# The end of token group 0 in another order, and three loads of group 3 issued sooner, in a kernel for block-wise attention with decay and an MLP

## The chip, the cores and the metric

The kernel runs on one core of one Trainium2 chip. The metric is the device time of one execution in microseconds (us); lower is better. Engines are named as in the profile: PE is TensorE, DVE VectorE, ACT ScalarE, POOL GpSimd, SP SyncE. POOL and SP each issue DMAs in the order of the program; POOL's go through the software queue (queue 0), SP's through the hardware queue (queue 1).

## What is computed

Attention with decay over 4 sequences of 768 tokens, 8 heads of 64, in blocks of 64 tokens with a running state per head, then an MLP with an exact GELU on the 3072 tokens (512 to 2048 and back to 512).

```python
for b in range(nb):                                   # nb = 12 blocks of 64 tokens
    intra = einsum('bhic,bhjc->bhij', qb, kb) * Dmask[None]
    intra = einsum('bhij,bhjd->bhid', intra, vb)
    inter = einsum('bhid,bhde->bhie', qb * lam_pow[None], kv_state)
    out[:, :, sl] = intra + inter
    kv_state = lam_block * kv_state + einsum('bhsd,bhse->bhde', kb * rev_pow[None], vb)
x = out.transpose(0, 2, 1, 3).reshape(3072, 512)
h = x @ w_in
out = (0.5 * h * (1 + erf(h / sqrt(2)))) @ w_out
```

## The kernel before

**Tiling.** A chunk is 128 tokens of one sequence (two blocks), a group is the same 128 tokens of all four sequences: chunks 4g to 4g+3 are group g, and there are six groups. While PE computes the MLP of group g, it also does the attention of group g+1 (in part g+2), in pieces put between blocks of the MLP. Nothing is scheduled automatically: each engine does its instructions in the order in which the program writes them.

**The MLP** (`mlp`, from L430) is a list of named blocks. `a`, `b`, `m` and `l` blocks are the first matmul (L439, L456) with GELU on ACT; `p0` to `p15` are the second matmul, four matmuls of 512 columns each (L478). In group 0 the `p` blocks go round the four output tiles, so that the four tiles end in `p12`, `p13`, `p14` and `p15`, and ACT copies each out (L467). In group 1 `a0` to `a3` use only chunks 4 and 5 and are half as wide.

**The attention of a chunk n** needs, in this order:
- loads of k and q (`load`, L71, POOL; for chunks 4 to 7 q comes for two chunks at once) and of V for a whole group in four DMAs (`load_blocks`, L106, POOL). They change the type from fp32 to bf16. A load waits for the semaphore that the load eight issues before it uses too.
- the transposes of k and q, tile `kqT`: for chunks 4 to 7 by PE in `both_transposed` (L248 and L252, 20 small matmuls into one PSUM bank; then a copy of the k half by DVE, L254, and of the q half by ACT, L255, one after the other, since both read one bank); from chunk 8 on by SP's DMA transposes in `request` (L259, L260).
- V times the decay, tile `vd`: `decay_v`, L282, on POOL.
- k in an order by blocks, tile `k2`: two copies `same` (L269) and two `other` (L273), on various engines. `values(n)` is `decay_v` and `same` on POOL, `keys(n)` is `other` on DVE.

**A visit(f, d)** (L349 and on) issues, interleaved pair by pair, chunk d's scores (8 pairs) and then its states (8 pairs, from `vd` and `k2`) and chunk f's outputs (16 pairs, from `kqT`, the masked scores `sm`, V, the state and the mid state `mid`). All matmuls are recorded at L347. After it DVE does the mask of d (L293), the first sum for the state (L308), then a copy to `mid` (L310 on ACT for chunks 4 to 7, L312 on DVE later), and "empties" f: x_t gets the outputs times a decay (L339). With `first=True` the emptying of f stands ahead of d's mask on DVE, else after the first sum.

**Order.** `run_blocks` (L519) walks the blocks; `ahead` and `plan_of` name what is put ahead of a block, on whichever engines. The lines around the change are those of group 0's second matmul (L590 to L602) and of `plan_of(1)` (L622 to L645), with n = 8: `m9` visit(None, 8), `m14` visit(8, 9), `p4` visit(9, 10), `p9` visit(10, 11), `p14` visit(11, 12). In group 2 `m0` has values(13), `m7` visit(12, 13), and `m15` visits chunk 13 with 14 and 15. `fetch` (L613) issues the loads of k and q of two chunks; where the first of these begins a group, V of that group too (L618).

Buffers: ten for k, ten for q from chunk 8 on, three for V of a group, six each for `kqT`, `vd`, `k2` and for output tiles, four PSUM banks for scores, states, outputs and transposes in turn.

Of the kernel before, what the change touches and what calls it, by code (L numbers as in the profile page):

```python
# [15 lines left out]
def kernel(  # L16
# [10 lines left out]
    nc = tc.nc  # L27
# [26 lines left out]
    def bank(shape, dtype, tag, name):  # L54
        return ps.tile(shape, dtype, tag=tag, name=name, bufs=BANKS[tag])

    def half(i):
        return slice(i * 64, (i + 1) * 64)
# [157 lines left out]
    live = {}  # L216
# [25 lines left out]
            dst, src = (t.rearrange(f"d hp ({o}) -> d hp p j", j=2) for t, o in ((c.qT, "p j"), (t_ps, "j p")))  # L242
        (nc.scalar.copy if eng is nc.scalar else eng.tensor_copy)(dst, src)

    def both_transposed(c):
        t_ps = bank([128, 2, HP, C], BF16, "at", "t_ps")
        for hp in range(HP):
            nc.tensor.transpose(t_ps[:, 0, hp, :], c.k[:, 2 * hp:2 * hp + 2, :], ident)  # L248
        for hp in range(HP):
            for j in range(2):  # L250
                for hi in range(2):
                    nc.tensor.transpose(t_ps[half(hi), 1, hp, half(j)], c.q[:, 2 * hp + hi, j, :],  # L252
                                        ident[half(0), half(0)])
        nc.vector.tensor_copy(c.kT, t_ps[:, 0])  # L254
        nc.scalar.copy(c.qT.rearrange("d hp (p j) -> d hp p j", j=2),  # L255
                       t_ps[:, 1].rearrange("d hp (j p) -> d hp p j", j=2))

# [27 lines left out]
    def scores(c):  # L285
        sc = c.sc = bank([128, 2, HP, L], F32, "at", "sc_ps")
        return [[(sc[half(hi), u, hp, :], c.kT[half(hi), hp, u * L:(u + 1) * L],
                  c.qT[half(hi), hp, u * L:(u + 1) * L], True) for hi in range(2)]
                for u in range(2) for hp in range(HP)]

    def mask(c):
        c.sm = work_pool.tile([128, 2, HP, L], BF16, tag="sm", name="sm")
        nc.vector.tensor_mul(c.sm, c.sc, dmask)  # L293

    def states(c):
        kv = c.kv = bank([128, 2, HP, D], F32, "at", "kv_ps")
        us = range(2) if c.g < NG - 1 else range(1)
        return [[(kv[half(hi), u, hp, :], c.k2[half(hi), u, hp, :], vd[c.n][half(hi), u, hp, :], True)
                 for hi in range(2)] for u in us for hp in range(HP)]
# [20 lines left out]
    def outputs(c, tag="at"):  # L320
        o = c.o = bank([128, HP, C], F32, tag, "o_ps")
        pairs = []

        def inter(u, s):
            for hp in range(HP):
                pairs.append([(o[half(1 - hi), hp, u * L:(u + 1) * L], s[half(hi), hp, :],
                               c.qT[half(hi), hp, u * L:(u + 1) * L], False) for hi in range(2)])

        inter(0, state[c.n])
        for u in range(2):  # L330
            for hp in range(HP):
                pairs.append([(o[half(1 - hi), hp, u * L:(u + 1) * L], c.v[half(hi), u, hp, :],
                               c.sm[half(hi), u, hp, :], False) for hi in range(2)])
        inter(1, c.mid)
        pairs[0] = [(*p[:3], True) for p in pairs[0]]
        return pairs

    def empty(c):
        nc.vector.tensor_mul(xT[c.g][:, :, c.b * C:(c.b + 1) * C], c.o, lam_o)  # L339

    def issue(*lists):

        for i in range(max(map(len, lists))):
            for pairs in lists:
                if i < len(pairs):
                    for out_, lhsT, rhs, start in pairs[i]:
                        nc.tensor.matmul(out_, lhsT, rhs, start=start, stop=True, skip_group_check=True)  # L347

    def visit(f, d, first=False):  # L349
        f, d = (live[n] if n is not None else None for n in (f, d))  # L350
        lists = []
        if d:
            kv = states(d)
            lists.append(scores(d) + kv)
        if f:
            lists.append(outputs(f))
        issue(*lists)
        if d is None or f and (first or f.g > 1):
            empty(f)
            f = None  # L360
        if d:
            mask(d)
            next_states(d, lambda: f and empty(f))
# [197 lines left out]
    def request(*ns):  # L561
        for n in ns:
            dma_transposes(live[n])

    def same(n, eng):
        by_block(live[n], eng, None)

    def other(n):
        by_block(live[n], None, nc.scalar)

    def ahead_of_group_1():

        for n in range(B, 2 * B):
# [20 lines left out]
        "p2": [lambda: both_transposed(live[4])],  # L594
        "p8": [lambda: visit(None, 4)],
        "p10": [lambda: both_transposed(live[5]), lambda: other(5)],
        "p12": [lambda: visit(4, 5), lambda: other(6)],
        "p13": [lambda: both_transposed(live[6])],
        "p14": [lambda: same(7, nc.vector)],
        "p15": [lambda: both_transposed(live[7]), lambda: other(7), lambda: visit(5, 6, first=True),  # L600
                lambda: request(8)],
    })  # L602


# [1 line left out]
    def values(n):  # L606
        decay_v(n)
        by_block(live[n], nc.gpsimd, None)
# [4 lines left out]
    def fetch(*ns):  # L613
        ns = [n for n in ns if n < NG * B]
        for n in ns:
            ask(f"k{n} q{n}")
        if ns and ns[0] % B == 0 and ns[0] > 2 * B:
            ask(f"V{ns[0] // B}")  # L618
        for n in ns:
            begin(n)  # L620

    def plan_of(g):  # L622
        if g == 1:
            n = 2 * B
            return {
                "a0": [lambda: values(n), lambda: request(n + 1), lambda: store_held(slice(0, 2))],
                "a2": [lambda: visit(n - 2, n - 1, first=True)],
                "b2": [lambda: fetch(n + 2, n + 3)],
                "m4": [lambda: visit(n - 1, None)],
                "m5": [lambda: keys(n), lambda: request(n + 2, n + 3), lambda: store_held(slice(2, B))],  # L630
                "l0": [lambda: values(n + 1)],
                "m9": [lambda: visit(None, n)],
                "m10": [lambda: values(n + 2)],
                "m11": [lambda: keys(n + 1)],
                "m14": [lambda: visit(n, n + 1)],
                "m15": [lambda: values(n + 3), lambda: fetch(n + 4, n + 5), lambda: request(n + 4, n + 5)],
                "p0": [lambda: keys(n + 2)],
                "p4": [lambda: visit(n + 1, n + 2)],
                "p5": [lambda: fetch(n + 6, n + 7), lambda: values(n + 4)],
                "p6": [lambda: keys(n + 3), lambda: request(n + 6, n + 7)],  # L640
                "p9": [lambda: visit(n + 2, n + 3)],
                "p11": [lambda: keys(n + 4)],
                "p13": [lambda: fetch(n + 8, n + 9)],
                "p14": [lambda: visit(n + 3, n + 4)],
            }  # L645
        if g == NG - 1:
            return {}
        n = (g + 1) * B
        if g == 2:
            return {  # L650
                "m0": [lambda: values(n + 1)],
                "m2": [lambda: keys(n + 1)],
                "m7": [lambda: visit(n, n + 1)],
                "m8": [lambda: values(n + 2), lambda: request(n + 4, n + 5)],
                "m10": [lambda: keys(n + 2), lambda: values(n + 3)],
                "m13": [lambda: keys(n + 3)],
                "m15": [lambda: visits([n + 1], [n + 2, n + 3], ["mo1"])],
                "p0": [lambda: fetch(n + 6, n + 7), lambda: values(n + 4)],
                "p2": [lambda: request(n + 6, n + 7), lambda: values(n + 5)],
                "p8": [lambda: keys(n + 4), lambda: keys(n + 5)],  # L660
                "p12": [lambda: visits([n + 2, n + 3], [n + 4, n + 5], ["mh", "mh"]), lambda: values(n + 6)],
            }

        def each(act, *ns):
            for n in ns:
                if n < NG * B:
                    act(n)

        return {
            "m0": [lambda: fetch(n + 4, n + 5), lambda: values(n + 3)],  # L670
            "m4": [lambda: keys(n + 2), lambda: keys(n + 3)],
            "m8": [lambda: each(request, n + 4, n + 5)],
            "m12": [lambda: visits([n, n + 1], [n + 2, n + 3], ["mo0", "mo1"]), lambda: each(values, n + 4)],
            "p0": [lambda: fetch(n + 6, n + 7), lambda: each(values, n + 5)],
            "p4": [lambda: each(request, n + 6, n + 7)],
            "p8": [lambda: each(keys, n + 4, n + 5)],
            "p12": [lambda: visits([n + 2, n + 3], [n + 4, n + 5], ["mh", "mh"]), lambda: each(values, n + 6)],
        }
# [34 lines left out]
```

## Time and profile before

| What | Value |
|---|---|
| Median of 3 runs | 211.13 us (209.91 to 211.71) |
| The profiled execution | 210.78 us |
| Its span, first to last instruction | 208.9 us |
| PE busy | 197.0 us, 94% |
| POOL busy | 104.6 us, 50% |
| DMA packets, queue 0 and queue 1 | 74080 and 21152 |
| Granted TensorE clock | 0.999 |

The profile records one execution. A row of the timeline has the start, the time taken, the engine, the line, the operation, what it writes and reads, how often, and in brackets how long the engine sat idle before it and what ended that. A row of the waits has who waited for whom, the total in us, how often, and the longest. A row of the DMA queues has packets, megabytes, and the time of the packets as a share of the 16 DMA engines' time. Matmuls overlap, so the distance between two starts tells more than their busy times. Some matmul records are missing: where a row has one matmul fewer than the program, a distance that looks doubled is no stall.

### The profile page before, as it was taken

How to read it: one execution, taken by the hardware profiler on the slowest of the kernel's cores; microseconds unless marked ns; L12 is line 12 of the kernel's file. 1: busy time of each engine (PE TensorE's matmuls, PEld its weight loads, DVE VectorE, ACT ScalarE, POOL GpSimd, SP SyncE). 2: the span in 40 equal slices, each digit the busy share in tenths (PEclk: the TensorE clock that was granted, in tenths of full speed). 3: DMA queues.
4: the chain of work that ended last, by engine and by line, in shares of the span. 5: the costliest groups of instructions: out<-in, count | busy, mean ns of one | idle time of the engine just before them, and what ended most of it. 6: DMA issues, size and time to landing. Idle time of an engine off the chain costs nothing.

```text
span 208.9 us, 5536 instructions
## 1 busy us (share of the span) xinstructions
PE 197.0 (94%) x2380; PEld 101.9 (49%) x2409; DVE 86.5 (41%) x188; ACT 87.6 (42%) x159; POOL 104.6 (50%) x148
## 2 busy tenths in 40 slices
PE   7689999998999998999999999999999999999992
PEld 2446444555854543444545445445445445444461
DVE  3789504365825564727783904905106002000000
ACT  5386661056656211356221464311565211765120
POOL 8989746897999723999299629800000000000000
PEclk9999999999999999999999999999999999999999
DMA  5999999999999999999999999544100021100121
GB/s 56 151 169 196 206 190 174 190 161 123 103 173 232 147 128 142 134 160 221 141 109 163 198 192 73 37 119 135 50 0 6 0 100 53 50 0 0 50 100 54
DMA packets 95256, 24.48 MB, mean 117 GB/s; under 512 B 86912, under 2 KB 92288, under 8 KB 95232
## 3 DMA queue, kind: packets, MB, share of 16 engines
q0 software_dynamic: 74080, 13.64, 90.0%
q1 hardware_dynamic: 21152, 10.50, 27.0%
q8 instruction: 19, 0.31, 0.7%
q14 instruction: 5, 0.04, 0.1%
HBM read 27.27 MB, written 6.29 MB: 161 GB/s over the span
## 4 chain that ended last, share of the span: by engine, by line
PE 58%; DMA 20%; POOL 18%; issue 2%; ACT 0%; POOLq 0%
PE h_ps L439 26%; PE o_ps L478 25%; DMA vg_t<-in_v_dram 14%; POOL vd L282 4%; DMA w_in_t<-in_moe_w_in_dram 4%; DMA v_t<-in_v_dram 3%; POOL kq_t L82 3%; POOL vg_t L106 2%; POOL k L269 2%; POOL q_t L71 2%; PE o_ps L489 2%; POOL k_t L71 2%; PE o_ps L347 2%; POOL w_in_t L126 1%; PE sc_ps L347 1%
## 5 line engine op out<-in xcount | busy, mean ns | idle before, releaser
L439 PE MATMUL h_ps<-x_t,w_in_t 128*128 128x512 bf16 (+3 forms) x396 | 83.7, 363 | 0.8
L478 PE MATMUL o_ps<-w_out_t,g_t 128*128 128x512 bf16 x354 | 80.9, 379 | 1.3 <-issue 0.6
L448 ACT ACTIVATE g_t<-h_ps 128x512 bf16<-128x512 f32 (+1 forms) x96 | 56.1, 591 | 30.9 <-PE h_ps L439 30.8
L439 PEld LDWEIGHTS <-w_in_t 128*128 128x128 bf16 x408 | 38.7, 98 | 41.5 <-issue 0.4
L478 PEld LDWEIGHTS <-g_t 128*128 128x128 bf16 x368 | 35.0, 98 | 41.1 <-issue 0.2
L467 ACT COPY o_sb<-o_ps 128x512 f32<-128x512 f32 (+1 forms) x25 | 14.2, 568 | 64.8 <-PE o_ps L478 59.4
L339 DVE TENSOR_TENSOR x_t<-o_ps,lam_o 128x512 bf16<-128x512 f32 x24 | 15.8, 687 | 59.6 <-PE o_ps L347 59.6
L282 POOL TENSOR_TENSOR vd<-vg_t,lam_v 128x512 bf16<-128x512 bf16 x20 | 21.0, 1051 | 19.1 <-DMA vg_t<-in_v_dram 11.3
L71 POOL DMA_DIRECT2D k_t<-in_k_dram x20 | 18.1, 905 | 2.0 <-DMA w_out_t<-in_moe_w_out_dram 1.5
L293 DVE TENSOR_TENSOR sm<-sc_ps,dmask 128x512 bf16<-128x512 f32 x20 | 13.2, 682 | 11.4 <-PE sc_ps L347 11.4
L106 POOL DMA_DIRECT2D vg_t<-in_v_dram x20 | 16.6, 852 | 1.5 <-DMA w_in_t<-in_moe_w_in_dram 1.5
L71 POOL DMA_DIRECT2D q_t<-in_q_dram x16 | 14.4, 898 | 2.5 <-DMA q_t<-in_q_dram 2.5
L269 POOL COPY k<-k_t 64x256 bf16<-64x256 bf16 x36 | 15.1, 419 | 1.0
L273 DVE COPY k<-k_t 64x256 bf16<-64x256 bf16 x34 | 12.0, 353 | 0.6
L347 PEld LDWEIGHTS <-kqT 64*64 64x64 bf16 (+1 forms) x352 | 7.7, 106 | 6.5 <-issue 6.0
L347 PE MATMUL sc_ps<-kqT 64*64 64x64 bf16 (+1 forms) x352 | 10.3, 197 | 0.4 <-issue 0.3
L347 PE MATMUL kv_ps<-vd,k 64*64 64x64 bf16 x288 | 8.6, 194 | 1.6 <-POOL k L269 1.0
L318 DVE TENSOR_TENSOR state<-t,lam_c 128x256 bf16<-128x256 f32 x16 | 9.0, 564 | 0.6
L347 PE MATMUL o_ps<-sm,vg_t 64*64 64x64 bf16 x320 | 9.0, 194 | 0.0
L516 PE MATMUL idle_ps<-idle 128*128 128x512 bf16 x22 | 7.2, 453 | 1.3 <-DVE idle L153 1.2
L126 POOL DMA_DIRECT2D w_in_t<-in_moe_w_in_dram x12 | 7.5, 699 | 0.9 <-DMA v_t<-in_v_dram 0.9
L347 PEld LDWEIGHTS <-vg_t 64*64 64x64 bf16 x320 | 7.1, 107 | 0.7 <-issue 0.7
(73 smaller groups left out, 128.5 us busy)
## 6 DMA issues: line engine op xcount, KB each, us to landing
out_dram<-o_sb SPq DMA_DIRECT2D x23, 256.0 KB, 4.4
k_t<-in_k_dram POOLq DMA_DIRECT2D x20, 128.0 KB, 6.6
vg_t<-in_v_dram POOLq DMA_DIRECT2D x20, 128.0 KB, 9.4
w_out_t<-in_moe_w_out_dram POOLq DMA_DIRECT2D x4, 512.0 KB, 10.8
q_t<-in_q_dram POOLq DMA_DIRECT2D x16, 128.0 KB, 6.5
w_in_t<-in_moe_w_in_dram POOLq DMA_DIRECT2D x8, 128.0 KB, 5.4
w_in_t<-in_moe_w_in_dram POOLq DMA_DIRECT2D x4, 256.0 KB, 6.4
kq_t<-in_k_dram POOLq DMA_DIRECT2D x4, 128.0 KB, 4.5
```

What stands on the lines that cost most here:

```text
L71: nc.gpsimd.dma_start(t, dram[name][b, :, g * C:(g + 1) * C, :].rearrange("h si d -> si h d"))
L106: nc.gpsimd.dma_start(t[half(hi), u], src[hi, s:s + L])
L269: same.tensor_copy(c.k2[half(hi), hi], k_r[half(hi), :, hi, :])
L273: copy(c.k2[half(hi), 1 - hi], k_r[half(1 - hi), :, hi, :])
L282: nc.gpsimd.tensor_mul(vd[n], of_group(n), lam_vb)
L293: nc.vector.tensor_mul(c.sm, c.sc, dmask)
L339: nc.vector.tensor_mul(xT[c.g][:, :, c.b * C:(c.b + 1) * C], c.o, lam_o)
L347: nc.tensor.matmul(out_, lhsT, rhs, start=start, stop=True, skip_group_check=True)
L439: nc.tensor.matmul(hs[kf][:, lo:up], w_in_t[:, ki, kf * 128:(kf + 1) * 128], x_t[:, ki, lo:up], start=(ki == 0 and lo == 0), stop=(ki == N ...
L448: nc.scalar.activation(g_t[:, kf, :up], hs[kf][:, :up], ACT.Gelu)
L467: nc.scalar.copy(o_sb, ps_)
L478: nc.tensor.matmul(om[io], g_t[:, kf, io * C:(io + 1) * C], w_out_t[:, kf, :], start=(kf == 0), stop=(kf == NK2 - 1))
```

## The change

In group 0's second matmul, with PE's order written out:

| | before | after |
|---|---|---|
| ahead of p11 | | visit(4, 5) |
| ahead of p12 | visit(4, 5) | |
| ahead of p13 | transposition of 6 | |
| ahead of p14 | | transposition of 6 |
| ahead of p15 | transposition of 7, visit(5, 6) | visit(5, 6), transposition of 7 |

The copies of chunk 6's and 7's k (`other(6)`, `same(7)`, `other(7)`) move along. For chunk 7 the k half of the transposition is copied by ACT (`nc.scalar`) instead of DVE; on ACT it stands behind the copy to `mid` of chunk 6 and ahead of chunk 7's q half.

In group 1's plan (n = 8) the loads of k and q of chunks 12 and 13 and of V of group 3, and SP's transposes of 12 and 13, move from ahead of `m15`, behind values(11), to ahead of `l0`, behind values(9). In POOL's queue these eight DMAs pass values(10) and values(11); on SP the order of instructions stays the same. Ahead of `p5` values(12) and the loads of chunks 14 and 15 change places: values(12), which needs V of group 3, is now first. Directly behind these loads on POOL come those of chunks 16 and 17 and V of group 4 (ahead of `p13`), then values(13). No instruction is added or taken away.

```diff
-    def both_transposed(c):
+    def both_transposed(c, eng=nc.vector):
...
-        nc.vector.tensor_copy(c.kT, t_ps[:, 0])
+        (nc.scalar.copy if eng is nc.scalar else eng.tensor_copy)(c.kT, t_ps[:, 0])
...
         "p10": [lambda: both_transposed(live[5]), lambda: other(5)],
-        "p12": [lambda: visit(4, 5), lambda: other(6)],
-        "p13": [lambda: both_transposed(live[6])],
-        "p14": [lambda: same(7, nc.vector)],
-        "p15": [lambda: both_transposed(live[7]), lambda: other(7), lambda: visit(5, 6, first=True),
-                lambda: request(8)],
+        "p11": [lambda: visit(4, 5), lambda: other(6)],
+        "p14": [lambda: both_transposed(live[6]), lambda: same(7, nc.vector), lambda: other(7)],
+        "p15": [lambda: visit(5, 6, first=True), lambda: both_transposed(live[7], nc.scalar), lambda: request(8)],
...
-                "l0": [lambda: values(n + 1)],
+                "l0": [lambda: values(n + 1), lambda: fetch(n + 4, n + 5), lambda: request(n + 4, n + 5)],
...
-                "m15": [lambda: values(n + 3), lambda: fetch(n + 4, n + 5), lambda: request(n + 4, n + 5)],
+                "m15": [lambda: values(n + 3)],
...
-                "p5": [lambda: fetch(n + 6, n + 7), lambda: values(n + 4)],
+                "p5": [lambda: values(n + 4), lambda: fetch(n + 6, n + 7)],
```

## The prediction

> **What bounds the kernel now.** I read the page's busy times first, then the waits of PE between 40 and 100 us, then the timelines of PE, POOL and ACT around them, and last the DMA queues by window. All times are us from the start of the one profiled execution. Chunk n's transposition is called tn, its scores, states and outputs come in visit(a, b).
>
> The page and the waits: TensorE is busy 94% of the span, and between 40 and 100 us little makes it wait.
>
> ```profile
> PE 197.0 (94%) x2380; PEld 101.9 (49%) x2409; DVE 86.5 (41%) x188; ACT 87.6 (42%) x159; POOL 104.6 (50%) x148
> ```
> ```profile
> PE kv_ps L347 <- POOL k L269: 1.0, 1, 1.0
> PE kv_ps L347 <- issue: 0.6, 1, 0.6
> PE t_ps L252 <- DMA q_t<-in_q_dram: 0.3, 1, 0.3
> ```
>
> So at most about 2.5 us can be won here. From start to start, less the usual distance, the three cost more than their idle time: t6 0.44 (45.94, its q landed late), 0.71 at 49.73 in visit(5,6) (no semaphore is waited for), 1.40 at 83.25 to 83.70 in visit(11,12), where the states of chunk 12 wait for POOL.
>
> The timeline of POOL shows why: the decay of chunk 12's V at 81.81 waited 6.59 us for V of group 3, issued at 65.94 to 69.23 behind the decays and copies of chunks 10 and 11.
>
> ```profile
> 56.80 1.04 POOL L282 TENSOR_TENSOR vd<-vg_t,lam_v 128x512 bf16<-128x512 bf16 x1
> ...
> 58.71 1.04 POOL L282 TENSOR_TENSOR vd<-vg_t,lam_v 128x512 bf16<-128x512 bf16 x1
> ...
> 62.41 0.91 POOL L71 DMA_DIRECT2D k_t<-in_k_dram  x1
> ...
> 65.94 3.29 POOL L106 DMA_DIRECT2D vg_t<-in_v_dram  x4
> 69.17 0.95 POOL L71 DMA_DIRECT2D k_t<-in_k_dram  x1
> ...
> 81.81 1.04 POOL L282 TENSOR_TENSOR vd<-vg_t,lam_v 128x512 bf16<-128x512 bf16 x1 [6.59 <-DMA vg_t<-in_v_dram]
> 82.81 0.85 POOL L269 COPY k<-k_t 64x256 bf16<-64x256 bf16 x2
> 83.60 0.92 POOL L71 DMA_DIRECT2D k_t<-in_k_dram  x1
> ...
> 87.14 3.29 POOL L106 DMA_DIRECT2D vg_t<-in_v_dram  x4
> 90.50 1.04 POOL L282 TENSOR_TENSOR vd<-vg_t,lam_v 128x512 bf16<-128x512 bf16 x1
> 91.49 0.85 POOL L269 COPY k<-k_t 64x256 bf16<-64x256 bf16 x2
> ```
>
> The last two rows are as tight as the stall: chunk 13's copies end at 92.34, and visit(12,13) (from 91.83) needs the second of them for the second half of chunk 13's states; PE goes on at 92.39 after 0.13 of stall. POOL's own chain is thus the second bound here.
>
> ACT around group 0's end (t5's and t7's copies, and a copy of chunk 6's state):
>
> ```profile
> 42.48 0.58 ACT L255 COPY kqT<-t_ps 128x512 bf16<-128x512 bf16 x1 [1.92 <-DVE kqT L254]
> 43.09 0.82 ACT L273 COPY k<-k_t 64x256 bf16<-64x256 bf16 x2
> ...
> 49.30 0.58 ACT L255 COPY kqT<-t_ps 128x512 bf16<-128x512 bf16 x1 [0.47 <-DVE kqT L254]
> ...
> 51.80 0.41 ACT L310 CAST mid<-t 128x256 bf16<-128x256 f32 x1 [1.08 <-DVE t L308]
> ```
>
> **Part 1: group 0's end.** I follow PE to the first scores of visit(6,7), which start at 51.86 now. A block of four matmuls takes 0.865 (eight: 46.31 to 48.04).
>
> visit(4,5) goes one block forward, from 43.74 to 42.88. But t5's copies and other(5) on ACT do not move: the two copies of k run 43.09 to 43.91, and the states of chunk 5 now start at 44.01. They can start at 43.97 at the earliest, so PE stands still for 0.82 of the 0.865 and the visit ends 0.04 sooner, at 44.37. DVE and ACT behind it, other(6) too, keep their times.
>
> Then p11 to p13, three blocks, end at 44.37 + 2.60 = 46.97, and t6 starts there; its q landed at 45.89, so the stall of 0.44 is gone. From t5's start (41.22) to the end of ACT's copy (43.06) it is 1.84, with 0.06 to the matmul 1.90; the transposes and one block take 1.66. So visit(5,6) finds kqT of chunk 6 at 46.97 + 1.90 = 48.87 and waits 0.24. same(7) on DVE and other(7) on ACT lie behind these copies and beside PE's block: nothing waits for them before visit(6,7).
>
> visit(5,6) then takes its first-to-last-start 0.51 (as visit(4,5)): 49.38. DVE begins 0.27 later; `first=True` puts empty(5), mask and t1 ahead of ACT's mid(6), 1.65 after DVE began (50.15 to 51.80): 51.30. On ACT t7's k copy now stands behind that mid: 0.31 to the next instruction, then two copies of 0.58 each. That the k copy on ACT costs as much as ACT's q copy is no guess, the first stage's k copies on ACT took 585 ns, on DVE 418. So kqT of chunk 7 is ready at 51.30 + 0.31 + 1.16 = 52.77, and visit(6,7) starts at 52.83 at the latest of its conditions. PE itself would be there at 52.05 (from 49.54: t7 0.69, p15 0.865, a0 and a1 together as much) or at 52.76, if the 0.71 of visit(5,6) recurs in the dense run of visit and t7. The trace does not say what that stall is: between 0 and 0.71, it is covered by this wait either way. **Part 1: 52.8 - 51.86 = +0.9** (0.5 if mid comes sooner, 1.2 if both this wait and some of the 0.71 show).
>
> **Part 2: the loads.** In POOL's queue the four loads of chunks 12 and 13 and the four of V pass two values() (1.9 each): they start at 58.66 instead of 62.41, 3.75 sooner, and delay values(10) and values(11) by 8 x 0.86 = 6.9, to ends of 67.4 and 69.3; visits needing them come at 71.6 and 76.8, so this is hidden with 4 us to spare. SP's order stays the same; its transposes of 12 and 13 start when the loads land. No buffer or earlier load holds them back: V uses a third buffer, k a tenth.
>
> The loads of 14 and 15 go the other way, behind values(12), which waits for V. Call V's landing L (81.50 now, 13.13 after the last issue). POOL then does, in rows of now: 0.31 to the decay, values(12) 1.79, four loads 3.53, the next four loads and V 6.90, values(13) 1.84: **14.4 from L to the second copy of chunk 13.** Before, the four loads lay in the time that POOL waited for V, and only 10.8 followed L. So each us that V comes sooner is first eaten by the 3.53: the copies end sooner than now only if L < 78.0.
>
> PE, if nothing waits, passes that point at 92.39 + 0.9 - 1.40 - 0.13 = 91.76. So the change costs max(-0.63, L - 78.0); the floor holds for L below 77.3. The stall in visit(11,12) itself is gone if L + 2.1 < 83, L < 80.9. k of 14 is issued at L + 2.1 and lands some 4.7 later (as k of 12: 62.41 to 67.08), so SP starts its transposes near 85.4 instead of 82.84, and the four take some 12 (82.84 to 95.3 now): 97.5, and the visit to 14 and 15 is at 99.7: hidden, by 2 us. The stores behind them on SP (89.47) come later; nothing on PE waits for those while six output buffers last. The waits of the loads of 14 and 15 for a load eight issues earlier (1.48 and 0.99 at 71.60 and 74.35) go, inside POOL's wait for V. The last load of V of group 4, at L + 11.4, must in turn find q of 15 landed, issued at L + 4.8: with the 4.7 to 9.0 of these loads 0 to 2.4; I take 0, since queue 0 is empty at L, and keep the rest for the range.
>
> L is the unknown. Lower end: the last issue 3.75 sooner with the same 13.13 gives 77.75; lower still if fewer of the standstills recur (77.0 to 79.6: 614 packets, cause not shown), say 75. Upper end: 81.50, if the DMA engines have no time to give. Between: queue 0 moved nothing from 62.7 to 64.7, now filled, which gives 79.5. I take **L = 78.6**, midway between 77.75 and 79.5: -0.63 is missed and the sum is 78.6 - 78.0 = **+0.6 us**.
>
> Which queue gives way is seen in the DMA view of 73.3 to 77.0, when two or three transposes of queue 1 were outstanding (one issued at 67.22 landed at 78.0):
>
> ```profile
> q0 software_dynamic: 3761, 0.47, 280.1%
> q1 hardware_dynamic: 258, 0.06, 18.5%
> ```
>
> **The sum.** The profiled execution took 210.78 (span 208.9 and 1.9 around), 0.35 below the median 211.13 and inside 209.91 to 211.71. 210.78 + 0.6 = **211.4**.
>
> **Rivals.**
> - *V early, only PE's floor counts* (L up to 77.3): 210.78 - 0.63 = 210.15. For it: without the standstills the rate of 73.3 to 77.0 (1016 packets of queue 0 per us) moves the 8192 packets from 62.7 in 8 us. Against: transposes and stores take their part. 0.24.
> - *V no sooner*: the loads and the transposes of chunks 10 to 13 take turns, everything that preceded V still does, L stays near 81.5, and the loads of 14 and 15 are added behind it: 81.5 - 78.0 = +3.5, 214.3. It decides from L = 80.1 on. For it: from 62.7 to 64.7 the engines were not idle, queue 1 moved 1666 packets. Against: the view above, 258 packets of queue 1 to 3761. 0.23. The Trainium skill, DMA: Bandwidth & Descriptors, section on queues, rings and completion order, says that each engine goes round between the queues that have work, a packet at a time; by that rule this rival would hold, at 214.3. The trace agrees only in part: 3017 to 1270 packets from 57.0 to 62.7, but 15 to 1 later.
> - *Queue 1 starves*: with queue 0 full from 62.7 to about 75, the transposes of chunk 10 (1024 packets, none served by 62.7) get 70 per us as in that view and land about 75; visit(9,10) at 72.5 waits 2.5: 0.9 + 2.5 - 1.53 = +1.9, 212.7. Against: 223 per us from 57.0 to 62.7 lands them by 68. 0.09.
> - *Group 0's waits do not arise* and L is below 75.3: -0.44 - 0.71 - 1.53 = -2.7, 208.1. Against: the ACT rows above. 0.06.
>
> **The numbers.** L between 77.3 and 80.1, my forecast, has 0.38. About 1% (2.1 us) is what a measurement of this kernel can tell from no change. Faster by more: 0.06. Slower by more: 0.23, and half of the starving case: 0.28. Within: 0.66. The range leaves out the fast case below and the end of the slow one: 209.6 (210.15 less the scatter) to 214.0.
>
> **What would show it.** Part 1: a PE wait of about 0.8 before visit(4,5)'s states, released by ACT L273; the wait for t6's q gone; a wait before the scores of chunk 7, released by ACT; visit(6,7) near 52.8. Part 2: loads of chunk 12 at 58.7; L, and decay of chunk 13 some 12.5 after it; no wait at visit(11,12); a wait for POOL L269 at visit(12,13) of L - 77.3. I am wrong if L falls outside 77 to 80, if visit(6,7) starts before 52.3, or if a visit to chunks 9 to 11 waits for its transposes.

## The result, and the profile after

| | before | after |
|---|---|---|
| Median | 210.89 us (209.91 to 211.71, 4 runs) | 217.50 us (217.33 to 217.72, 4 runs) |
| Ratio after to before, with its 95% interval | | 1.0316 [1.0269, 1.0362] |
| The profiled execution, its span | 210.78, 208.9 us | 217.72, 215.9 us |
| PE busy, granted TensorE clock | 197.0 us, 0.999 | 200.1 us, 0.988 |

The change costs 3.2%, where no change that can be measured was forecast; 217.5 lies 3.5 us above the end of the range. The ratios in this text leave out runs more than 1.5% above the fastest of their kernel, so a ratio can differ a little from the quotient of two medians.

The page of after: the busy times, and the row of the granted clock in 40 slices of 5.4 us each.

```profile
PE 200.1 (93%) x2380; PEld 103.0 (48%) x2409; DVE 84.8 (39%) x187; ACT 88.1 (41%) x160; POOL 104.3 (48%) x148
PEclk9999999999999999996999999999999999999998
```

PE is busy 3.1 us longer with the same number of matmuls, and one slice (97.1 to 102.5 us) has a granted clock of 0.6, where the same row of before has nines throughout. PE's waits from 35 to 120 us, in us in total, times and the longest:

```profile
PE kv_ps L347 <- POOL k L269: 4.3, 2, 3.2
PE sc_ps L347 <- ACT kqT L255: 1.0, 3, 0.6
...
PE kv_ps L347 <- ACT k L273: 0.4, 1, 0.4
```

The wait for POOL's copies of k, which the loads sent sooner might have removed, has grown from 1.0 to 4.3 us and comes twice. The timeline of PE has each of them, in brackets at the end of a row:

```profile
44.29 0.22 PE L347 MATMUL sc_ps<-kqT 64*64 64x64 bf16 x2 [0.17 <-ACT kqT L255]
...
45.14 0.21 PE L347 MATMUL kv_ps<-vd,k 64*64 64x64 bf16 x1 [0.40 <-ACT k L273]
...
50.00 0.22 PE L347 MATMUL sc_ps<-kqT 64*64 64x64 bf16 x2 [0.17 <-ACT kqT L255]
...
53.88 0.22 PE L347 MATMUL sc_ps<-kqT 64*64 64x64 bf16 x2 [0.63 <-ACT kqT L255]
...
85.21 0.22 PE L347 MATMUL kv_ps<-vd,k 64*64 64x64 bf16 x2 [1.11 <-POOL k L269]
...
97.38 0.22 PE L347 MATMUL kv_ps<-vd,k 64*64 64x64 bf16 x2 [3.15 <-POOL k L269]
...
97.84 0.22 PE L347 MATMUL o_ps<-kqT,mid 64*64 64x64 bf16 x2
```

These are, in turn, the scores and the states of visit(4,5), the scores of visit(5,6) and of visit(6,7), the states of visit(11,12) and those of visit(12,13); the last row is where PE goes on in visit(12,13) once the second copy of chunk 13's k is there, which was at 92.39 in before. POOL's timeline shows what these states wait for:

```profile
58.97 0.92 POOL L71 DMA_DIRECT2D k_t<-in_k_dram  x1
...
62.49 3.29 POOL L106 DMA_DIRECT2D vg_t<-in_v_dram  x4
...
68.75 0.85 POOL L269 COPY k<-k_t 64x256 bf16<-64x256 bf16 x2
83.78 1.04 POOL L282 TENSOR_TENSOR vd<-vg_t,lam_v 128x512 bf16<-128x512 bf16 x1 [14.18 <-DMA vg_t<-in_v_dram]
84.76 0.85 POOL L269 COPY k<-k_t 64x256 bf16<-64x256 bf16 x2
85.55 0.93 POOL L71 DMA_DIRECT2D k_t<-in_k_dram  x1
...
92.56 3.32 POOL L106 DMA_DIRECT2D vg_t<-in_v_dram  x4
95.95 1.04 POOL L282 TENSOR_TENSOR vd<-vg_t,lam_v 128x512 bf16<-128x512 bf16 x1
96.94 0.84 POOL L269 COPY k<-k_t 64x256 bf16<-64x256 bf16 x2
```

The loads start 3.44 us sooner (58.97 for 62.41) and pass the decays and copies of chunks 10 and 11, as the change says. But V of group 3 lands no sooner: **L = 83.47**, before 81.50; its last load, issued at 64.91, took 18.56 us instead of 13.13. POOL then stands for 14.18 us with the loads of chunks 14 to 17 and V of group 4 behind the decay, and when V is there, all of them lie between values(12) and values(13). The first copy of chunk 13 ends at 97.33 and lets the states begin; the second ends at 97.78. From 83.5 to 87.5 us the DMA engines move 66 packets in all: the queue that was too full until L is empty right after it.

How the time is built up, from starts in the two traces:

| Point on PE | before | after | difference |
|---|---|---|---|
| First matmul of the MLP (L439), unchanged code ahead | 16.36 | 17.00 | +0.64 |
| t5, unchanged code ahead | 41.22 | 42.40 | +1.18 |
| Scores of visit(6,7) | 51.86 | 53.88 | +2.02 |
| States of visit(11,12) | 83.25 | 85.21 | +1.96 |
| Visit(12,13), behind the second copy of chunk 13 | 92.39 | 97.84 | +5.45 |
| Visit of chunk 13 with 14 and 15 | 99.65 | 106.78 | +7.13 |
| Span | 208.9 | 215.9 | +7.0 |

All is lost by 106.78. The late start (1.18) and group 0 (2.02 - 1.18 = 0.84) lie ahead of the wait for V, which swallows such delays (group0_only below). What counts is the late second copy of chunk 13 (+5.45) and, from there to the next visit, 1.7 more (8.94 for 7.26 us) in which PE waits for nothing. There the clock is the reason. The windows of after (length; busy us of PE, PEld, DVE, ACT and POOL; then granted clock, DMA share and GB/s):

```profile
94.00:96.00 2.00, 0.23 (x31) 0.12 (x16) 0.00 (x0) 0.49 (x1) 1.94 (x4) 1.00 2.08 166
96.00:98.00 2.00, 0.50 (x32) 0.39 (x32) 0.00 (x0) 0.00 (x0) 1.86 (x4) 1.00 2.03 159
98.00:100.00 2.00, 1.78 (x19) 0.76 (x13) 1.73 (x4) 0.11 (x1) 1.86 (x4) 0.56 2.68 134
100.00:102.00 2.00, 2.00 (x7) 0.76 (x6) 1.95 (x4) 0.89 (x2) 1.94 (x4) 0.58 1.17 155
```

While PE waits it is granted full speed, for nothing; when it has gone on, the clock is halved from 98.25 to 101.67, 3.413 us. Half of that is 1.71 us, which agrees with the 1.7 lost.

### The profile page after: what moved, and what is told of

The parts are those of the page before. It is cut to its first block, busy times and chain, and to the rows that moved or that the text cites. A ratio compares the mean times of both kernels' runs of the same rounds, so it can differ in the third digit from the quotient of the medians.

```text
span 215.9 us, 5535 instructions
## 1 busy us (share of the span) xinstructions
PE 200.1 (93%) x2380; PEld 103.0 (48%) x2409; DVE 84.8 (39%) x187; ACT 88.1 (41%) x160; POOL 104.3 (48%) x148
## 4 chain that ended last, share of the span: by engine, by line
PE 52%; DMA 23%; POOL 20%; issue 3%; ACT 0%; POOLq 0%
PE o_ps L478 24%; PE h_ps L439 24%; DMA vg_t<-in_v_dram 16%; POOL vd L282 4%; DMA w_in_t<-in_moe_w_in_dram 4%; POOL vg_t L106 3%; POOL q_t L71 3%; DMA v_t<-in_v_dram 3%; POOL k_t L71 3%; POOL kq_t L82 3%; POOL k L269 2%; PE o_ps L489 2%; PE o_ps L347 2%; POOL w_in_t L126 1%; PE sc_ps L347 1%
## 5 line engine op out<-in xcount | busy, mean ns | idle before, releaser
L439 PE MATMUL h_ps<-x_t,w_in_t 128*128 128x512 bf16 (+3 forms) x396 | 85.1, 368 | 1.0 <-issue 0.2
L439 PEld LDWEIGHTS <-w_in_t 128*128 128x128 bf16 x408 | 39.1, 99 | 42.6 <-issue 2.7
L71 POOL DMA_DIRECT2D q_t<-in_q_dram x16 | 14.4, 901 | 0.0
L273 DVE COPY k<-k_t 64x256 bf16<-64x256 bf16 x34 | 10.4, 307 | 0.6
L516 PE MATMUL idle_ps<-idle 128*128 128x512 bf16 x22 | 8.4, 513 | 1.3 <-DVE idle L153 1.2
L347 PEld LDWEIGHTS <-k 64*64 64x64 bf16 x288 | 6.7, 107 | 5.8 <-POOL k L269 4.9
L318 DVE TENSOR_TENSOR state<-t,lam_c 128x256 bf16<-128x256 f32 x16 | 8.2, 512 | 0.6
```

What stands on the lines that cost most here:

```text
L71: nc.gpsimd.dma_start(t, dram[name][b, :, g * C:(g + 1) * C, :].rearrange("h si d -> si h d"))
L273: copy(c.k2[half(hi), 1 - hi], k_r[half(1 - hi), :, hi, :])
L439: nc.tensor.matmul(hs[kf][:, lo:up], w_in_t[:, ki, kf * 128:(kf + 1) * 128], x_t[:, ki, lo:up], start=(ki == 0 and lo == 0), stop=(ki == N ...
```

## The experiments

The theory after the result: the DMA engines serve the two queues in turn, so V lands where it did or later however soon it is asked for (*taking turns*), and the loads of chunks 14 to 17 behind values(12) then put the second copy of chunk 13 some 14.3 us behind it (*the queue*). The rivals: group 0's new order is what costs (*group 0*); V was late in this execution by its scatter; or the halved clock is the main loss (*the clock*). Ratios are to before on the same chip, with 95% intervals.

### The old order ahead of p5 back: p5_back

```diff
 # against after
-                "p5": [lambda: values(n + 4), lambda: fetch(n + 6, n + 7)],
+                "p5": [lambda: fetch(n + 6, n + 7), lambda: values(n + 4)],
```

> The changed kernel, with the loads of chunks 14 and 15 again ahead of values(12). Queue theory (the loss is POOL's chain from V's landing L to the copies of chunk 13, 14.3 us with the four moved loads in it, and a halved clock that follows from the wait): the chain is 10.8 us again, so with L near 83.5 the copies end near 94.3 instead of 97.8, the wait at visit(12,13) shrinks from 3.15 us to under 0.5, the clock stays full, and the time falls by 3.5 + 1.7 to about 212.3. Landing theory (V lands late because the DMA engines are shared, and the order on POOL does not matter): stays near 217.5.

Measured: 212.25 us (209.85 to 215.8, 10 runs), 1.004 [0.9995, 1.0084]; 5.2 us less than after. One line of order carries most of the loss: of 6.6 us over before 1.4 are left. The profiled execution is the longest of the ten (215.8): V landed at 85.24, visit(11,12) waited 2.6 us and the clock was halved behind it. A late V alone can thus still cost much; with the old order it does so seldom (two of the ten runs are above 213). No trace shows one of the other eight; that their wait at visit(12,13) is short follows from their time alone.

### That line alone: p5_only

The same line as in the change, made in before.

> The kernel before, with only values(12) put ahead of the loads of chunks 14 and 15. Queue theory: V still lands near 81.5, the copies of chunk 13 end at 81.5 + 14.4 = 95.9 instead of 92.3, so +3.5 us, 214.4, and up to 216.1 if the wait halves the clock for 3.4 us. Landing theory: V lands as before, 210.9 within 0.5.

Measured: 214.99 us (218.46, 215.20, 214.78 and 210.57; no ratio, since the four lie too far apart). The profiled execution is the longest, and has POOL's and PE's rows of after, to some hundredths:

```profile
83.79 1.04 POOL L282 TENSOR_TENSOR vd<-vg_t,lam_v 128x512 bf16<-128x512 bf16 x1 [12.56 <-DMA vg_t<-in_v_dram]
...
96.98 0.85 POOL L269 COPY k<-k_t 64x256 bf16<-64x256 bf16 x2
```
```profile
97.42 0.22 PE L347 MATMUL kv_ps<-vd,k 64*64 64x64 bf16 x2 [3.17 <-POOL k L269]
```

L is 83.48, the copies end at 97.83, 14.35 later; the clock was halved from 98.70 to 102.12. So the line makes the loss by itself when V is late; no trace shows the run of 210.57, in which it did not. V was late here though its loads were asked for no sooner than in before (67.88 to 70.40). In after all four runs are long (217.33 to 217.72), so its time is not the chance of one execution.

### Group 0's order alone: group0_only

The lines of group 0 and of the transposition (those of `both_transposed` and of `p11` to `p15` in the change), made in before.

> The kernel before, with only the new order of group 0's end. Both theories: visit(6,7) starts 0.8 to 0.9 us later. If V's landing and POOL's chain are what ends last, the wait at visit(11,12) shrinks by as much, and the time is 210.9 to 211.2. If the cost of group 0's end carries through to the end, 211.7.

Measured: 211.12 us (10 runs), 0.9991 [0.9956, 1.0025]. PE's rows for visit(6,7) and visit(11,12):

```profile
52.87 0.22 PE L347 MATMUL sc_ps<-kqT 64*64 64x64 bf16 x2 [0.61 <-ACT kqT L255]
...
83.67 0.22 PE L347 MATMUL kv_ps<-vd,k 64*64 64x64 bf16 x2 [0.55 <-POOL k L269]
```

The waits for ACT are there, and what they cost is taken off the wait for V behind them (0.55 for 1.0). *Group 0* is out as the cause.

### The loads alone: loads_only

```diff
 # against before; p5 stays as before
-                "l0": [lambda: values(n + 1)],
+                "l0": [lambda: values(n + 1), lambda: fetch(n + 4, n + 5), lambda: request(n + 4, n + 5)],
...
-                "m15": [lambda: values(n + 3), lambda: fetch(n + 4, n + 5), lambda: request(n + 4, n + 5)],
+                "m15": [lambda: values(n + 3)],
```

> The kernel before, with only the loads of chunks 12, 13 and V of group 3 at l0 (values(12) stays behind the loads of 14 and 15, group 0 as before). Sharing theory (loads and transposes take turns on the DMA engines, so loads asked for 3.75 us sooner only move the transposes of 10 to 13 among them): V's first request is at 58.7, its landing still at 81 to 83, its latency 17 us instead of 13; time as before, 210.9 within 0.7. Rival, the prediction's term (L = 78.6): the wait at visit(11,12) is gone and the time is about 209.5.

Measured: 211.21 us (10 runs), 1.0029 [0.9985, 1.0073]. POOL's rows:

```profile
59.99 0.92 POOL L71 DMA_DIRECT2D k_t<-in_k_dram  x1
...
63.52 3.29 POOL L106 DMA_DIRECT2D vg_t<-in_v_dram  x4
...
84.43 1.04 POOL L282 TENSOR_TENSOR vd<-vg_t,lam_v 128x512 bf16<-128x512 bf16 x1 [8.72 <-DMA vg_t<-in_v_dram]
```

V was asked for 2.42 us sooner than in before (63.52 for 65.94) and landed at 84.12, 2.62 later. The trace is of the longest of the ten runs (213.45), but the median, too, is that of before: asking sooner brought nothing.

### The transposes of chunks 10 to 13 taken out: no_transposes

```diff
 # against after
         for n in ns:
-            dma_transposes(live[n])
+            if 10 <= n < 14:
+                nc.vector.memset(live[n].kqT, 0.0)
+            else:
+                dma_transposes(live[n])
```

The eight transposes are left out and zeros take their place, so the scores of these four chunks come out as zeros, and their visits wait for no transpose; queue 0 and POOL's order stay as in after.

> The changed kernel without the eight DMA transposes of chunks 10 to 13: DVE fills their tiles with zeros instead, so the attention of these chunks is left out in part. Sharing theory (V of group 3 lands late because the transposes of 10 to 13 take turns with the loads): 8 x 512 packets less, which take about 5 us at the 770 a microsecond seen when queue 1 was alone, so V lands at 76 to 79 instead of 81 to 85, the waits at visit(11,12) and visit(12,13) go or fall below 1 us, about 211.5. Rival (the software queue moves a load in 2 us whatever else runs): V still at 81 to 85, 214 or more.

Measured: 210.01 us (8 runs), 0.9964 [0.9932, 0.9997]. POOL's rows, where the decay found V there and waited for PE instead:

```profile
62.36 3.29 POOL L106 DMA_DIRECT2D vg_t<-in_v_dram  x4
...
74.37 1.04 POOL L282 TENSOR_TENSOR vd<-vg_t,lam_v 128x512 bf16<-128x512 bf16 x1 [4.83 <-PE o_ps L347]
```

L is 74.06, 9.4 us sooner than in after, more than expected. Only queue 1's work was taken away, so this is what it takes from queue 0. The DMA queues (packets, megabytes, share) show it: from 63.5 to 74 us here,

```profile
q0 software_dynamic: 8184, 1.03, 154.4%
q1 hardware_dynamic: 433, 0.79, 22.6%
```

and from 66 to 80 us first in before, then in after:

```profile
q0 software_dynamic: 8167, 1.03, 149.7%
q1 hardware_dynamic: 1633, 0.85, 60.4%
```
```profile
q0 software_dynamic: 6695, 0.84, 94.6%
q1 hardware_dynamic: 4478, 1.56, 79.9%
```

Queue 1 moved 2.7 times as many packets while V was under way, and that is no chance of one execution: from 66 to 80 us it has 4029 to 4478 in the five traces with the loads sooner and k and q first, 1633 to 2781 in the three with the loads where they were. A reason shows in the stretch from 62.7 to 64.7 us. In before queue 0 moved nothing there, and queue 1 moved 1666 packets. In after loads fill it; the two queues in this stretch:

```profile
q0 software_dynamic: 1028, 0.13, 101.8%
q1 hardware_dynamic: 377, 0.33, 67.2%
```

The transposes of chunks 10 and 11, sent 1.8 to 2.0 us later in this execution than in before, landed 3.3 to 5.5 us later: at 67.69 to 73.67 instead of 64.41 to 68.14, and so beside the loads of V. Those of chunks 12 and 13 landed 1.1 to 3.1 us sooner than in before, the last at 82.48, and so came into the same stretch. What queue 0 gained ahead of V, queue 1 took back later. Which four of the eight transposes weigh more, no run tells.

*Taking turns* holds in this sense: the work of queue 1 delays V. The Trainium skill, DMA: Bandwidth & Descriptors, section on queues, rings and completion order, has the rule that the prediction weighed, that each engine goes round between the queues that have work. The trace agrees, with V 9.4 us sooner once queue 1's work is gone. The row that spoke against it, 258 packets to 3761, was one stretch of before and not the rule.

### PE kept at work ahead of visit(12,13): warm and warm14

Eight, and then fourteen, matmuls of 512 columns on zeros, ahead of the visit whose states wait. They change no output.

```diff
 # against after (warm14: 14)
+    def idle_matmuls(n):
+        t = bank([128, 512], F32, "mo0", "idle2_ps")
+        for _ in range(n):
+            nc.tensor.matmul(t, idle[:, :128], idle, start=True, stop=True)
...
-                "m7": [lambda: visit(n, n + 1)],
+                "m7": [lambda: idle_matmuls(8), lambda: visit(n, n + 1)],
```

> The changed kernel, with eight matmuls on zeros (1.7 us, more work than the program's) put ahead of visit(12,13), inside PE's wait of 3.15 us. If the wait is what halves the clock for 3.4 us, the clock stays full and the time falls by about 1.7 us to 215.8. If the halved clock has another cause, it stays near 217.5; if PE does not really wait there, 219.

> The changed kernel with fourteen matmuls on zeros (3.0 us) ahead of visit(12,13), instead of eight, with which 1.4 us of wait were left and the clock still halved. If it is the share of PE's idle time in a window of 3.4 us that halves the clock, it stays full now, and the time falls by about 1.7 us, to 215 to 216 with V near 83; if matmuls on zeros do not count, or the cause is another, the clock halves near 97 to 99 as before and the time is 217.5 or, where V lands sooner than 82, up to 1 us more than the wait would give.

Measured: warm 215.85 us (4 runs), 1.0241 [1.0152, 1.033]; warm14 214.64 us (4 runs), 1.018 [1.0114, 1.0247]. The number expected of warm came for another reason: 1.4 us of wait were left and the clock was halved all the same (96.83 to 100.25), but V had landed at 81.88. That run settles nothing by itself. Beside warm14 (L 81.22, no wait left) it does. The window from 98 to 100 us, in warm and then in warm14:

```profile
98.00:100.00 2.00, 2.00 (x6) 0.70 (x5) 1.93 (x4) 0.71 (x2) 1.86 (x4) 0.50 1.49 248
```
```profile
98.00:100.00 2.00, 2.00 (x11) 0.94 (x10) 1.92 (x5) 1.29 (x3) 1.94 (x4) 1.00 1.44 284
```

At half the clock PE has 6 matmuls in these two microseconds, at the full one 11. The states of visit(12,13) begin at 95.82 and 95.88 in the two, and PE goes on behind the second copy at 96.28 and 96.01; the visit to chunks 14 and 15 starts at 105.22 and 103.25. From the second copy on that is 8.94 and 7.24 us, as in after and before (8.94 and 7.26): the halved clock costs 1.7 us, a part of the loss and not the main one. With eight matmuls it does not come every time: by the granted clock of each run two of warm's four had it (0.989; 216.10 and 217.39 us) and two did not (1.0 and 0.999; 214.58 and 215.60 us).

### V ahead of k and q: v_first, v_first_l0_p5, v_first_after

In the loads of group 3 the four of V are put ahead of k and q of chunks 12 and 13: in before, in before with the change's part 2, and in the whole change.

```diff
 # in fetch(); ask() issues the loads that a string names
+        v_first = ns and ns[0] == 3 * B
+        if v_first:
+            ask(f"V{ns[0] // B}")
         for n in ns:
             ask(f"k{n} q{n}")
-        if ns and ns[0] % B == 0 and ns[0] > 2 * B:
+        if ns and ns[0] % B == 0 and ns[0] > 3 * B:
```

> The kernel before, with the four loads of V of group 3 ahead of those of k and q of chunks 12 and 13 in the same place. Queue and sharing theory: V passes four loads of about 2 us each in the software queue and lands near 74, so the wait of 1.4 us at visit(11,12) goes; k and q of 12 land some 5 us later, and their transposes at 82 to 84, against 81.85 where visit(11,12) wants them: between 209.4 and 211.5. If V's landing were set by something other than its place in the queue: 210.9.

> The kernel before with V of group 3 first, then k and q of 12 and 13, all asked for at l0, and values(12) ahead of the loads of 14 and 15 (the changed kernel's two moves of loads, but V at the head; group 0 as before). Queue theory: V lands near 71, POOL waits for it 2 us instead of 14, the 14.4 us chain ends near 86, far ahead of visit(12,13); no wait for POOL at either visit: 209.4 if the transposes of 12 land before 82. Rival (the new order on POOL is bad in itself): 214 or more.

> The whole change, but with the four loads of V of group 3 ahead of those of k and q of chunks 12 and 13. Queue theory: V lands near 71 to 73, the 14.4 us chain is done near 87, nothing waits for POOL at visit(11,12) or visit(12,13), the clock stays full, and only group 0's end is left of the cost: 210.87 - 1.4 - 0.1 + 0.8 = 210.2. Rival (group 0's end or the order on POOL costs more than its 0.8): 212 or more.

Measured (10 runs each): v_first 209.94 us, 0.9959 [0.9916, 1.0002], L 75.74; v_first_l0_p5 210.97 us, 1.0001 [0.9964, 1.0037], L 71.24; v_first_after 211.23 us, 1.0013 [0.9984, 1.0042], L 73.38. POOL's rows of v_first_after:

```profile
58.73 3.31 POOL L106 DMA_DIRECT2D vg_t<-in_v_dram  x4
...
73.55 1.04 POOL L282 TENSOR_TENSOR vd<-vg_t,lam_v 128x512 bf16<-128x512 bf16 x1 [4.18 <-DMA vg_t<-in_v_dram]
...
87.73 0.84 POOL L269 COPY k<-k_t 64x256 bf16<-64x256 bf16 x2
```

The whole change, its new order ahead of p5 included, costs nothing once V is there in time: L + 14.3 is 87.7, and the copies ended at 88.57 (0.91 of wait for k of chunk 12 came in between), ahead of their visit. So the new order of POOL's instructions does harm only where V is late. But v_first_l0_p5 and v_first_after missed 209.4 and 210.2: the wait for V goes, and the time does not fall as far as the wait was long.

### Looking for a better kernel: v_first_t6, v_mid_t6

Both are before with t6 moved ahead of `p14`, where its q has landed; v_first_t6 with V first, v_mid_t6 with V between chunk 12's loads and chunk 13's.

```diff
 # against before; v_mid_t6 has in place of v_first:
         for n in ns:
             ask(f"k{n} q{n}")
+            if n == 3 * B:
+                ask("V3")
...
-        "p13": [lambda: both_transposed(live[6])],
-        "p14": [lambda: same(7, nc.vector)],
+        "p14": [lambda: both_transposed(live[6]), lambda: same(7, nc.vector)],
```

> A try for a better kernel: the kernel before with V of group 3 ahead of k and q of 12 and 13 (where it asked for them before), and the transposition of 6 put ahead of p14 instead of p13, all else of group 0 as before. The wait of 0.44 for t6's q goes; from t6 to visit(5,6) PE has 0.69 + 0.865 + 0.69 = 2.25 us of work against the 1.90 that kqT of chunk 6 takes, so no new wait. Expected 0.4 below the 209.9 of V first alone: 209.5. If the wait for q is only moved to another instruction, 209.9.

> A second try for a better kernel: the kernel before with the four loads of V of group 3 between those of chunk 12 and those of chunk 13 (V passes two loads, k and q of 12 keep their place), and the transposition of 6 ahead of p14. V passes two loads of about 2 us and lands near 77 instead of 81.5, the copies of chunk 12 end near 80, ahead of visit(11,12) at 82; k and q of 13 land near 81, ten us before visit(12,13). All three waits (0.44, 1.4, 0.13) go and none takes their place: 209.0. If the transposes of 12 come as late as with V first (a wait of 1.1 there), 210.0.

Measured (12 runs each): v_first_t6 210.36 us, 0.9966 [0.9929, 1.0004]; v_mid_t6 210.55 us, 0.998 [0.9952, 1.0008]. Neither is faster than before by more than the measurement can tell. In v_first_t6 the wait has moved; PE's row at the scores of chunk 12:

```profile
83.16 0.22 PE L347 MATMUL sc_ps<-kqT 64*64 64x64 bf16 x2 [1.15 <-DMA kqT<-q_t]
```

What V gains in the queue, q of chunk 12 and its transposition lose. In v_mid_t6 (L 77.46) the three waits that it was to remove (0.44, 1.4 and 0.13) are gone. The stall in visit(5,6) that waits for no semaphore is still there, and it is PE's longest from 35 to 120 us:

```profile
51.16 0.19 PE L347 MATMUL kv_ps<-vd,k 64*64 64x64 bf16 x1 [0.66 <-issue]
```

Its profiled execution began late as well: the first matmul of the MLP at 17.48, before at 16.36. Over all traces this start lies between 16.36 and 18.01, mostly near 17.0; before's profiled execution had the earliest. As long as PE waits for V, whose landing the queues set, a late start is taken off that wait, as group 0's 0.84 was in group0_only; without the wait it shows in full. By this account the 1.40 of stall in before's trace was worth less than 1.40 in a usual run; it rests on one trace of each kernel, and no run tests it.

## Why the prediction was wrong, step by step

| Step, as predicted | Predicted | Measured in after | |
|---|---|---|---|
| From t5 to the states of visit(4,5) | 41.22 to 43.97: 2.75 | 42.40 to 45.14: 2.74 | right, but for where PE waits |
| Part 1, scores of visit(6,7) | +0.9 | +0.84 over t5's | right, and hidden |
| First load of chunk 12 | 58.7 | 58.97 | right |
| "I take **L = 78.6**" | 78.6 | 83.47 | **failed** |
| From L to the second copy of chunk 13 | 14.4 | 97.78 - 83.47 = 14.31 | right |
| Wait at visit(11,12), gone if L + 2.1 < 83 | gone | 1.11, L + 1.74 = 85.21 | follows L |
| Loads of 14 and 15 later: hidden | 0 | 0, no wait at 106.78 | right |
| TensorE's clock | no term | +1.7 | **missing** |

**The failed step** is the landing of V: "Upper end: 81.50, if the DMA engines have no time to give", and 78.6 taken between 77.75 and 79.5. Both ends of the inner range supposed that V's packets would go out in the time in which queue 0 had moved nothing, or sooner by the 3.75 us. That time was not free. In before queue 1 moved 1666 packets in it; in after queue 0 took it (1028 packets to 377), and the transposes of chunks 10 and 11 were moved later instead, beside V. The prediction had the 1666 packets among the grounds of a rival and left them out of L. It left out, too, that queue 0 was not empty when the loads came (chunk 11's q landed at 64.10, before at 62.68), and that the transposes of chunks 12 and 13, started by the landing of their loads, fall into the time in which V is under way. 81.50 was not an upper end: with k and q first and all transposes, L is 83.47, 85.24, 84.12, 81.88 and 81.22 in the traces with the loads sooner, and 81.50, 81.92 and 83.48 in those with the loads where they were.

**The formula was right, the value in it was not.** "The change costs max(-0.63, L - 78.0)" gives +5.5 for 83.47; behind the second copy of chunk 13 PE goes on 5.45 later. The rival *V no sooner* (0.23) is what happened, its mechanism shown by no_transposes and loads_only; it gave 214.3, as it held L at 81.5 and the clock at full speed. 2.0 more from L and 1.7 from the clock make it 218.0, against 217.72 in this execution. The condition that it named, L above 80.1, was met in every trace with k and q first and with all transposes.

**The missing term.** Before was granted full speed throughout its work (0.999), and the prediction had no line for what follows a long wait. The Trainium skill, TensorE: Matmul & The Clock Gate, part 1 on the clock gate, says that the array falls to half its clock after at least one idle window of some 3.4 us and that the window runs freely. The traces agree with the window and its length (below), but PE was not idle for all of it: a wait of 3.15 us was enough in after, and one of 1.45 in warm.

**What the forecast did not need.** Part 1 was worked out to a tenth and counted in full, though it lay ahead of a wait for a transfer whose end the queues set; group0_only (0.9991) shows it absorbed. One condition in it was passed over: visit(4,5) was put at 42.88, though by the 1.90 that Part 1 itself counts from t5's start to the scores it could not start before 43.12. So PE waited 0.17 for t5's copy and 0.40 for the copies of k, where one wait of about 0.8 was named; the states came when forecast all the same.

What is open: why L scatters by some 2 us either way from execution to execution of one order; why the three parts do not add (group0_only and loads_only within 0.3%, p5_only +4.1 us at its median, all together +6.6); and what the stalls at "issue" are.

## What to carry to other kernels

Before a load is put earlier, ask who uses the DMA engines at that time and what the landing starts: here the time in which one queue stood still was used by the other's transposes, which then came later and took turns with the very transfer that was to come sooner. An instruction that waits for a transfer should have nothing behind it in its queue that could go ahead of it; the order of loads within the queue (V first, L 71 to 76) moved the landing; with k and q ahead of V the time of asking did not. A wait on PE of some 3 us is to be priced with the slower microseconds that can follow it (1.7 us here), and a stall that is read in one execution with how early that execution began.

## What the runs showed of the hardware

- **The clock is decided on a grid.** Where a trace has a stretch of halved clock amid its work, it begins a whole number of 3.413 us after the clock first became full, and lasts 3.413 us (times in us; the last column is for the 3.413 us just before the halving):

| Trace | full from | halved from | distance | PE busy before it |
|---|---|---|---|---|
| after | 6.09 | 98.25 | 92.16 = 27 x 3.413 | 0.75 |
| p5_only | 6.54 | 98.70 | 92.16 = 27 x 3.413 | 1.17 |
| warm | 4.67 | 96.83 | 92.16 = 27 x 3.413 | 1.85 |
| p5_back | 5.85 | 87.77 | 81.92 = 24 x 3.413 | 0.69 |
| v_first | 6.37 | 16.61 | 10.24 = 3 x 3.413 | 1.50 |
| warm14 | 4.39 | 11.22 | 6.83 = 2 x 3.413 | 2.55 |

Other stretches of the grid with 2.0 and more stayed at full speed, but so did one of 1.76 (loads_only) and one of 1.85 (v_first_l0_p5), so that busy time as the trace has it, with some matmuls missing, gives no sharp limit. A wait of 1.4 us cost 1.7 us more in warm and nothing more in loads_only; what decided between them is not shown.

- **The two queues' shares differ from stretch to stretch**: 3761 packets to 258 from 73.3 to 77.0 us in before, 6695 to 4478 from 66 to 80 us in after. Why the first stretch was so one-sided, no run tells.
- **Stalls that wait for no semaphore** of 0.55 to 1.40 us show in six of the fourteen traces between 49.7 and 51.5 us, where a visit and a transposition stand close together (0.55 at 49.73 in before, 1.40 at 50.58 in v_first_l0_p5); in this stretch the others have none of over 0.5. The cause was not found.
